# One-hot places of a routed group compared column by column in a fused attention and mixture-of-experts kernel

## The chip, the cores and the metric

The kernel runs on one core of one Trainium2 chip. The time is device microseconds from a launch's start to its end; of several runs the median is given. Beside the runs there is one profiled execution, from which all rows below come.

## What is computed

A linear attention over random features, and behind it a layer that sends each token to one of eight experts.

```python
batch, n_heads, seq, head_dim = (8, 8, 576, 64)      # 4608 tokens of 512
...
q_p, k_p = (phi(q_s), phi(k_s))                      # exp of projections on 128 features
kv = np.einsum('bhsm,bhsd->bhmd', k_p, v)
z = np.sum(k_p, axis=2)
num = np.einsum('bhsm,bhmd->bhsd', q_p, kv)
den = np.einsum('bhsm,bhm->bhs', q_p, z)[..., None] + 1e-06
...
logits = x @ w_gate
e_idx = np.argmax(logits, axis=1)                    # one expert a token
...
for e in range(E):
    mask = e_idx == e
    h = np.maximum(x[mask] @ w1[e], 0.0)
    ye = h @ w2[e]
    out[mask] = gate_w[mask, None] * eom[mask, e, None] * ye
```

## The kernel before

The 4608 tokens are worked in four groups of nine columns of 128 tokens (`NSC` = 4, `NC` = 9). For each group the attention of its eight pairs of heads is computed and written to the table `rows` in HBM, and then the group is routed: the expert of each token is found, and each token gets a rank among the tokens of its expert. The experts' work is done in items of 128 tokens of one expert. An item gathers its tokens' rows with an indirect DMA (`gx`), turns them (`xt`), multiplies by both weights of its expert (`hA`, `hB`, `out`) and scatters the result (`os`, `put`). Items of the groups that are routed are worked while the attention of the next group is still under way, so that the tensor engine goes back and forth between attention and items; only the items of the last group stand alone at the end.

The order of all steps is written out by hand in one list (`ORDER`), and each engine issues its instructions in that order. A step of several links (`route`, `ranks`, `places`, `table`, `assign`, `lists`) is a Python generator; each `yield` ends a link, and the list puts links of different steps and of the attention between them.

The steps around the change, all on VectorE save the two matmuls:
- `ranks` (L1036) makes `rank`, nine numbers a lane, in PSUM, in a bank that the group's routing holds (`inner`). The key of a token is a whole number for its block of 128, plus a fraction of a place.
- `places` (L1053) has three links: L1056 rounds the rank to the key (`keys`, in SBUF), L1058 subtracts the key, which leaves the token's place within its block, and L1060 compares it with `iota` (0 to 127, less a half of 127, fp16, in SBUF). The result is `place`: for each of the group's nine columns a matrix of 128 x 128 in fp16 that has one 1 a token. It is one instruction of 1152 elements, with `iota` read nine times over and each rank read 128 times.
- `table`, `assign`, `controls` set up which block of which expert goes to which item, and `lists` (L1144) compares the keys with the items' keys and makes `r_itc`.
- `pid` (L1283, `indices`) multiplies `place` by `r_itc` on the tensor engine, nine matmuls for each group that is routed so far; `gi` (L1320) and `oi` (L1326) are the lists of tokens that come out, for the gather and the scatter. `oi` is also what frees the bank of `pid`.
- At the end of the kernel two buffers for results are laid over `place` (L1421).

GpSimd works beside VectorE in the attention: L580 (`xlo`), L728 (`es`), L742 (`vs`) and L893 (`xs`), TENSOR_TENSORs from SBUF to SBUF, and it issues the gathers and scatters (L1565, L1664). VectorE's cast of `xs` is L889; L512 splits weights; L458, L459, L621 and L625 belong to the start of the kernel.

Of the kernel before, what the change touches and what calls it, by code (L numbers as in the profile page):

```python
# [16 lines left out]
ALU = mybir.AluOpType  # L17
# [5 lines left out]
P = 128  # L23
# [5 lines left out]
NC = 9  # L29
# [364 lines left out]
def attention_moe(ctx: ExitStack, tc: tile.TileContext, kqt, kqn, v, om, wg, w1, w2, cf, cm, ci, out):  # L394
    nc = tc.nc
# [11 lines left out]
    tri, ones, iota, ident16 = (cmt[:, i, :] for i in range(4))  # L407
# [20 lines left out]
    place = const.tile([P, NSC * NC, P], F16, name="place")  # L428
# [499 lines left out]
    def small(nm, sh, dt=F32):  # L928
        return sb.tile([P, *sh], dt, tag="r_" + nm, name="r_" + nm, bufs=1)
# [123 lines left out]
    def places(j):  # L1053

        rank, key = rt[j]["rank"], keys[:, j * NC : (j + 1) * NC]
        nc.vector.tensor_scalar(key, rank, WHOLES, -WHOLES, ALU.add, ALU.add)  # L1056
        yield
        nc.vector.tensor_tensor(out=rank, in0=rank, in1=key, op=ALU.subtract)  # L1058
        yield
        nc.vector.tensor_tensor(  # L1060
            out=place[:, j * NC : (j + 1) * NC, :],
            in0=iota.unsqueeze(1).broadcast_to([P, NC, P]),
            in1=rank.unsqueeze(2).broadcast_to([P, NC, P]),
            op=ALU.is_equal,
        )

    tabs = {}

# [270 lines left out]
    def routing(j):  # L1339


        def chain(name, links, gen, after, **kw):
            plan.chain((name, j), ("DVE",), links, lambda: gen(j), after=after, **kw)

        first = [("lga", H * (j + 1) - 1), ("const", "st"), ("const", "cf"), ("const", "cm")]
        if j:
            first += [("places", j - 1), ("scales", j - 1)]
        old = [g for g in range(NG) if GROUPS[g] < j]
        chain("route", 5, route, first)
        plan.add(("counts", j), ("PE",), lambda: counts(j), after=[("route", j)], bank=("e", ("pos", j), [NC + 1, NE]))  # L1350
        chain("ranks", 4, ranks, [("counts", j)] + [("table", g) for g in old], frees=[("pos", j)])
        chain("places", 3, places, [("ranks", j)])
        chain("gates", 2, gates, [("route", j)])
        plan.add(("gate_exps", j), ("ACT",), lambda: gate_exps(j), after=[("gates", j)])
        chain("weigh", 4, weigh, [("gate_exps", j)])
        plan.add(("scales", j), ("SP",), lambda: save_scales(j), after=[("weigh", j)], tiles=[("scales", j)])
# [414 lines left out]
```

## Time and profile before

| | |
|---|---|
| median of 3 runs | 644.57 us (643.44 to 647.48) |
| the profiled execution | 648.04 us |
| its span, first to last instruction | 646.2 us |
| tensor engine busy | 584.8 us, 91% of the span |
| VectorE busy | 407.2 us, 63%, 1115 instructions |
| ScalarE busy | 417.0 us, 65% |
| GpSimd busy | 362.1 us, 56%, 263 instructions |
| mean granted clock of the tensor engine | 0.978 |

A busy share is a mean over stages. The tensor engine's work is not spread evenly: in the first sixth of the span it often stands, and in the last items the chain of waits ends in a scatter. Times in the rows are us from the start of the span.

### The profile page before, as it was taken

What the parts mean: (1) busy time and instruction counts of PE and PEld (TensorE: products, weight loads), DVE (VectorE), ACT (ScalarE), POOL (GpSimd) and SP (SyncE); (2) the same over time, 40 slices, a digit from 0 to 9 for tenths busy, and PEclk for the clock granted to TensorE, in tenths of its full rate; (3) what the DMA queues carried; (4) which work ended last, traced back from release to release, by engine and by line L of the source; (5) the groups of instructions that cost most, each with busy time, mean ns of one, the idle gap of its engine ahead of it and who ended that gap; (6) DMA issues with size and microseconds to landing.
All of it is one profiled execution on the core that took longest, in us unless ns stands there. A gap on an engine that the chain in (4) does not pass through costs nothing. (4 is left out here: it accounts for less than half of the span.)

```text
span 646.2 us, 21319 instructions
## 1 busy us (share of the span) xinstructions
PE 584.8 (91%) x8412; PEld 452.7 (70%) x8412; DVE 407.2 (63%) x1115; ACT 417.0 (65%) x970; POOL 362.1 (56%) x263
## 2 busy tenths in 40 slices
PE   5899865999999898999989999999998899999983
PEld 4777754866777676777757776876776576767763
DVE  5988999957687687655757865564883620521052
ACT  5788997888888777878768577777521611521151
POOL 3887264388867856968657767858442211212111
PEclk9999997899999999999989999999999999999998
DMA  8696999999998987789999958558957744824570
GB/s 307 211 330 223 301 243 254 200 229 247 276 333 179 207 231 202 194 232 251 164 317 205 232 145 169 123 130 211 298 153 207 213 83 117 307 55 94 127 265 16
DMA packets 147759, 133.74 MB, mean 207 GB/s; under 512 B 104607, under 2 KB 128545, under 8 KB 146337
## 3 DMA queue, kind: packets, MB, share of 16 engines
q1 hardware_dynamic: 141632, 112.19, 68.0%
q0 software_dynamic: 5984, 19.72, 9.8%
q8 instruction: 82, 1.34, 0.9%
q14 instruction: 61, 0.49, 0.2%
HBM read 88.59 MB, written 19.30 MB: 167 GB/s over the span
## 5 line engine op out<-in xcount | busy, mean ns | idle before, releaser
L705 ACT ACTIVATE ef<-pp,nb 128x128 f32<-128x128 f32 x576 | 164.4, 389 | 48.2 <-DVE nb L699 36.1
L688 DVE TENSOR_REDUCE pp<-pp 128x3 f32<-128x384 f32 x192 | 104.8, 560 | 53.6 <-PE pp L670 48.9
L728 POOL TENSOR_TENSOR es<-ef,es 128x1152 f16<-128x1152 f32 x44 | 104.4, 2381 | 34.6 <-ACT es L726 13.1
L1599 PE MATMUL ph<-xt,w1h 128*128 128x128 f16 (+1 forms) x2048 | 121.7, 217 | 0.7 <-PE ph L1599 0.3
L1599 PEld LDWEIGHTS <-w1h 128*128 128x128 f16 x2048 | 113.3, 98 | 5.9 <-issue 0.8
L1565 POOL DMA_INDIRECT gx<-rows,gi x38 | 40.6, 1068 | 134.1 <-ACTq L1532 64.7
L1610 DVE SCALAR_TENSOR_TENSOR hl<-ph,hh 128x512 f16<-128x512 f32 (+1 forms) x76 | 50.4, 663 | 100.5 <-ACTq L1532 75.1
L1632 PEld LDWEIGHTS <-hh 128*128 128x128 f16 x560 | 51.6, 98 | 58.2 <-issue 4.0
L1606 ACT ACTIVATE hh<-ph 128x512 f16<-128x512 f32 (+1 forms) x76 | 44.7, 590 | 70.6 <-PE ph L1599 54.3
L580 POOL TENSOR_TENSOR xlo<-xt,xhi 128x1152 f16<-128x1152 f32 x24 | 57.5, 2398 | 25.0 <-ACT xhi L577 24.4
L1599 PE MATMUL ph<-xt,w1l 128*128 128x128 f16 (+1 forms) x1024 | 66.5, 217 | 2.2 <-issue 2.2
L1632 PE MATMUL po<-w2h,hh 128*128 128x512 f16 x240 | 62.6, 383 | 3.2 <-ACT w2h L507 2.9
L1632 PE MATMUL po<-w2h,hl 128*128 128x512 f16 x240 | 62.2, 382 | 0.5 <-DVE hl L1610 0.5
L1632 PE MATMUL po<-w2l,hh 128*128 128x512 f16 x240 | 61.6, 379 | 0.0
L1599 PEld LDWEIGHTS <-w1l 128*128 128x128 f16 x1024 | 58.4, 98 | 3.1 <-issue 3.0
L1675 ACT ACTIVATE os<-po,gx 128x512 f32<-128x512 f32 (+1 forms) x36 | 24.7, 686 | 48.4 <-PE po L1632 44.8
L893 POOL TENSOR_TENSOR xs<-xf,xs 128x576 f16<-128x576 f32 x32 | 40.9, 1283 | 20.9 <-DVE xs L889 9.5
L726 ACT CAST es<-ef 128x1152 f16<-128x1152 f32 x44 | 50.9, 1162 | 1.6 <-ACTq L1527 0.7
L1632 PEld LDWEIGHTS <-hl 128*128 128x128 f16 x280 | 27.1, 99 | 35.5 <-DVE hl L1610 3.5
L854 PE MATMUL pn<-kvs,et 128*128 128x81 f16 x768 | 39.3, 203 | 6.1 <-DVE oi L1326 3.1
L854 PEld LDWEIGHTS <-et 128*128 128x128 f16 x768 | 33.9, 98 | 10.2 <-issue 5.1
L670 PEld LDWEIGHTS <-xhi 64*128 64x128 f16 x864 | 26.5, 95 | 15.2 <-issue 10.0
(207 smaller groups left out, 1036.4 us busy)
## 6 DMA issues: line engine op xcount, KB each, us to landing
r<-w SPq DMA_DIRECT2D x10, 2048.0 KB
xn<-kqn SPq DMA_DIRECT2D x31, 576.0 KB
xt<-kqt SPq DMA_DIRECT2D x31, 576.0 KB
rawv<-v SPq DMA_DIRECT2D x32, 325.0 KB
rows<-xs SPq DMA_DIRECT2D x16, 576.0 KB
r<-w SPq DMA_DIRECT2D x8, 512.0 KB
ef<-w SPq DMA_DIRECT2D x2, 512.0 KB
et<-w SPq DMA_DIRECT2D x2, 512.0 KB
```

The lines of the kernel that those rows point to most:

```text
L580: plan.add(("lo", u, x), ("POOL",), lambda t0=t0, t1=t1: nc.gpsimd.tensor_tensor(out=xl(u)[:, t0:t1], in0=xt32(u)[:, t0:t1], in1=xh(u)[:, ...
L688: nc.vector.tensor_reduce(out=spare(g, 0)[:, i], in_=banks["pp", 2 * u + i, g][:, 0:3, :], op=ALU.min, axis=AX.X)
L705: nc.scalar.activation(ef(2 * u + i)[:, c, :], banks["pp", 2 * u + i, g][:, c % 3, :], AF.Exp, bias=nb(u)[:, i, c : c + 1], scale=-SK)
L726: nc.scalar.copy(es(slot_es(n))[:, 0], ef(n))
L728: nc.gpsimd.tensor_tensor(out=es(slot_es(n))[:, 1], in0=ef(n), in1=es(slot_es(n))[:, 0], op=ALU.subtract)
L854: nc.tensor.matmul(pn[:, c - c0, :], a[:, c, :], w[:, :, 0 if c < 4 else 1], start=(i == 0 and c == c0), stop=(c == NC - 1 and i == len(op ...
L893: nc.gpsimd.tensor_tensor(out=x[:, :, P + o : P + o + D], in0=xf(u)[:, :, 0:D], in1=x[:, :, o : o + D], op=ALU.subtract)
L1565: return nc.gpsimd.indirect_dma_start(out=gx(n), out_offset=None, in_=rows[0 : (j + 1) * NC * P], in_offset=bass.IndirectOffsetOnAxis(ap=t ...
L1599: nc.tensor.matmul(ph[:, f4, 0:w_], w[qd][:, kk, fo : fo + P], xt(n)[:, x, 0:w_], start=(z == 0 and f4 == 0 and x == 0), stop=(z == 1 and ...
L1606: nc.scalar.activation(hh(n)[:, sl, 0:w_], banks["ph", n, g][:, :, 0:w_], AF.Relu)
L1610: nc.vector.scalar_tensor_tensor(out=hl(n)[:, sl, 0:w_], in0=banks["ph", n, g][:, :, 0:w_], scalar=0.0, in1=hh(n)[:, sl, 0:w_], op0=ALU.ma ...
L1632: nc.tensor.matmul(po, x(n)[:, f, :], w[f // 2][:, f % 2, :], start=(f == 0 and a == 0), stop=(f == FC - 1 and a == 2))
```

## The change

The difference of rank and key is written to a new small tile in SBUF (`lane`), where it used to overwrite the rank in PSUM. The one compare of all nine columns becomes nine compares of one column each: `iota` is the only tensor that is read, and the place of each lane comes in as the instruction's scalar, one number a lane. The three links and their places in the order stay as they are; the nine compares are all in the third link.

```diff
--- before.py
+++ after.py
@@ -1055,14 +1055,11 @@
         rank, key = rt[j]["rank"], keys[:, j * NC : (j + 1) * NC]
         nc.vector.tensor_scalar(key, rank, WHOLES, -WHOLES, ALU.add, ALU.add)
         yield
-        nc.vector.tensor_tensor(out=rank, in0=rank, in1=key, op=ALU.subtract)
-        yield
-        nc.vector.tensor_tensor(
-            out=place[:, j * NC : (j + 1) * NC, :],
-            in0=iota.unsqueeze(1).broadcast_to([P, NC, P]),
-            in1=rank.unsqueeze(2).broadcast_to([P, NC, P]),
-            op=ALU.is_equal,
-        )
+        lane = small("place", [NC])
+        nc.vector.tensor_tensor(out=lane, in0=rank, in1=key, op=ALU.subtract)
+        yield
+        for c in range(NC):
+            nc.vector.tensor_scalar(place[:, j * NC + c, :], iota, lane[:, c : c + 1], None, ALU.is_equal)
 
     tabs = {}
```

## Rows read from the trace of the kernel before

**Rows 1.** Busy time by stage: us, then busy (instructions) of PE, PEld, DVE, ACT, POOL; PEclk.

```profile
104.00:107.00 3.00, 0.24 (x3) 0.14 (x3) 2.93 (x13) 1.07 (x2) 2.48 (x2) 0.74 1.34 177
...
120.00:480.00 360.00, 343.99 (x5336) 262.83 (x5336) 249.08 (x697) 269.41 (x616) 258.52 (x170) 1.00 0.89 217
```

**Rows 2.** The compare: ns min/median/max, starts; VectorE's timeline (start us, us, instruction), three of four.

```profile
L1060 DVE TENSOR_TENSOR place<-cmt,rt x4: 1353/1353/1355, 100.8 to 479.2; 128x1152 f16<-128x1152 f16 x4
...
100.78 1.35 DVE L1060 TENSOR_TENSOR place<-cmt,rt 128x1152 f16<-128x1152 f16 x1
...
228.04 1.35 DVE L1060 TENSOR_TENSOR place<-cmt,rt 128x1152 f16<-128x1152 f16 x1
...
364.55 1.35 DVE L1060 TENSOR_TENSOR place<-cmt,rt 128x1152 f16<-128x1152 f16 x1
```

**Rows 3.** VectorE's timeline: TENSOR_SCALARs with a lane's scalar, and their followers.

```profile
106.01 0.22 DVE L1195 TENSOR_SCALAR rt<-cft,r_tot 128x8 f32<-128x8 f32 x1
106.14 0.56 DVE L688 TENSOR_REDUCE pp<-pp 128x3 f32<-128x384 f32 x1
...
485.79 0.43 DVE L1186 TENSOR_SCALAR ef<-ef,cft 128x864 f16<-128x864 f16 x1
486.14 0.16 DVE L1216 SCALAR_TENSOR_TENSOR r_lim<-state,rt 128x8 f32<-128x8 f32 x1
```

**Rows 4.** Durations of one cast; then timelines of VectorE and GpSimd around 248 and 18.

```profile
L889 DVE CAST xs<-xf x32: 478/484/2381, 28.2 to 471.5; 128x576 f16<-128x576 f32 x32
...
248.34 2.38 DVE L889 CAST xs<-xf 128x576 f16<-128x576 f32 x1
...
248.00 2.37 POOL L728 TENSOR_TENSOR es<-ef,es 128x1152 f16<-128x1152 f32 x1 [1.60 <-ACT es L726]
...
17.72 0.61 DVE L458 TENSOR_SCALAR wgh<-wgr 128x256 f16<-128x256 f32 x1
18.36 1.58 DVE L459 SCALAR_TENSOR_TENSOR wgl<-wgr,wgh 128x256 f16<-128x256 f32 x1
...
18.26 1.41 POOL L625 TENSOR_TENSOR sqt<-sqt 128x576 f32<-128x576 f32 x1
```

**Rows 5.** GpSimd's timeline beside the four compares.

```profile
101.78 4.69 POOL L580 TENSOR_TENSOR xlo<-xt,xhi 128x1152 f16<-128x1152 f32 x2
...
227.29 2.39 POOL L728 TENSOR_TENSOR es<-ef,es 128x1152 f16<-128x1152 f32 x1
231.64 2.38 POOL L580 TENSOR_TENSOR xlo<-xt,xhi 128x1152 f16<-128x1152 f32 x1 [1.96 <-ACT xhi L577]
...
365.29 2.38 POOL L580 TENSOR_TENSOR xlo<-xt,xhi 128x1152 f16<-128x1152 f32 x1
367.63 1.43 POOL L742 TENSOR_TENSOR vs<-rawv,vs 128x650 f16<-128x650 f32 x1
...
477.57 1.00 POOL L1664 DMA_INDIRECT out<-os,oi  x1 [0.30 <-issue]
```

**Rows 6.** Timelines of the tensor engine and VectorE: lists, `pid` and waits.

```profile
111.08 0.98 PE L854 MATMUL pn<-kvs,et 128*128 128x81 f16 x12 [3.14 <-DVE oi L1326]
...
233.04 0.45 DVE L1164 TENSOR_TENSOR r_itc<-r_eq,rt 128x288 f16<-128x288 f16 x1
...
233.79 0.60 PE L1287 MATMUL pid<-r_itc,place 128*128 128x16 f16 x18
...
367.58 0.17 DVE L868 TENSOR_SCALAR den<-pn 128x5 f32<-128x5 f32 x1 [0.44 <-PE pn L861]
...
370.20 0.66 DVE L1164 TENSOR_TENSOR r_itc<-r_eq,rt 128x486 f16<-128x486 f16 x1
...
371.33 0.84 PE L1287 MATMUL pid<-r_itc,place 128*128 128x18 f16 x27
```

**Rows 7.** The tensor engine's timeline at 331, and that stretch by stage (as rows 1).

```profile
331.38 1.96 PE L1632 MATMUL po<-w2h,hh 128*128 128x512 f16 x4 [2.94 <-ACT w2h L507]
...
331.00:334.00 3.00, 2.62 (x7) 0.83 (x7) 2.64 (x3) 3.00 (x4) 0.00 (x0) 0.50 1.14 330
```

## The prediction

> **What bounds the kernel now.** I read four views, in this order. First the table by stage (busy time of each engine in a stretch), to see which engine sets the pace where the change sits. From 120 to 480 us the tensor engine is busy 343.99 of 360.00 us [rows 1]: whatever holds it up in that stretch or ahead of it has almost no idle time later in which to be made up. Ahead of it, where the first of the four groups is routed, it is the other way round: from 104 to 107 us VectorE is busy 2.93 of 3.00 us and the tensor engine 0.24 [rows 1]. Second, the instructions that write `place`: the compare runs four times, 1353 to 1355 ns, never stretched [rows 2]. Third, VectorE's order of time, for what small instructions cost in a row [rows 3]. Fourth, GpSimd's order of time beside it, because some VectorE instructions have two very different durations and GpSimd's rows explain which [rows 4, 5].
>
> **What goes.** One TENSOR_TENSOR of 1152 elements, at 1.35 us a group [rows 2]. Neighbours on VectorE overlap: the row of 0.22 us at 106.01 is followed at 106.14 [rows 3], 0.09 before its end. So the old compare holds its queue for about 1.35 - 0.08 = 1.27 us. The subtraction stays one instruction of 9 elements; that it writes SBUF and no longer PSUM I cost at nothing: it stands in the same place of the queue, and its result is first read by the instruction that also reads it now.
>
> **What comes, with nothing in its way.** Nine TENSOR_SCALARs of 128 fp16 elements, each with a scalar of its lane. Two rows of that kind exist. With 8 elements the next instruction starts 0.13 us later; with 864 fp16 elements, both sides in SBUF, 0.35 us later [rows 3]. The slope is (0.35 - 0.13) / 856 = 0.26 ns an element, against 1.35 us / 1152 = 1.17 ns in the old compare: the one-source form runs about four elements for each one of the two-source form. A compare of 128 elements is 0.13 + 0.03 = 0.16 us, nine are 1.44 us, against 1.27: +0.17 a group. The bounds: if the fixed part were the 0.09 between 106.14 and its neighbour's end, nine would be about 1.08 (-0.19 a group); if they ran at the old 1.17 ns, 9 x (0.13 + 0.15) = 2.52 (+1.25 a group). I take 1.44, since the 864-element row has operands, scalar and type of the new ones.
>
> [...]
>
> **What is in its way.** The form that is quick is also the one that stops for GpSimd. The cast of `xs` (one source, SBUF to SBUF) takes 478 to 484 ns as a rule and 2381 at most; the longest starts at 248.34 and ends at 250.72, and GpSimd's TENSOR_TENSOR ran from 248.00 to 250.37 [rows 4]. The cast ended 0.35 after it, having waited for its end. The old compare, one of whose two inputs is in PSUM, ran 1354 ns four times, with GpSimd busy in three of them [rows 2, 5]. Nine TENSOR_SCALARs from SBUF to SBUF should behave as the cast does. And each asks anew: around 18 us a TENSOR_SCALAR ended at 18.33, GpSimd's next operation had started at 18.26, and the VectorE instruction of 18.36 ended at 19.94, 0.27 after GpSimd's end at 19.67 [rows 4]. A GpSimd operation that stands ready gets in between two VectorE instructions. [...]
>
> *First group, 100.78.* A GpSimd operation ends at 101.8 and two more, 4.69 us together, follow without idle time, to 106.47 [rows 5]. One or two compares get in at 101.8, one or two at about 104.1, the other five or six after 106.47: 106.5 + 6 x 0.16 + 0.1 for GpSimd's own delay = 107.6, where the old one let go at 100.78 + 1.27 = 102.05. That is +5.5 us. Behind it VectorE queues everything up to the list of places, the tensor engine's next work waits for VectorE (3.14 us at 111.08 [rows 6]), and VectorE has no idle time there [rows 1]. All 5.5 reach the end. If VectorE kept the port for all nine it would be 101.8 + 1.44 - 102.05 = +1.2.
>
> *Second group, 228.04.* GpSimd's operation ends at 229.68; the next starts at 231.64 after 1.96 idle [rows 5]. The nine run from 229.68 to 231.12, against 229.31: +1.8. `r_itc` ended at 233.49 and the tensor engine's `pid` began at 233.79 [rows 6], so 0.3 is covered and +1.5 is left.
>
> *Third group, 364.55.* GpSimd runs without a gap until 365.3, 367.67 and 369.06 [rows 5]. By the same alternation the last five or six compares come after 369.06: 369.06 + 0.96 + 0.1 = 370.1 against 365.82, +4.3. Cover: 0.44 idle at 367.58, and `r_itc` ended at 370.86 where `pid` began at 371.33, 0.47 [rows 6]. The tensor engine stands 3.4. [...] The 2.62 us of work in that stretch would have been half of it at full clock, 1.3; I add 1.0, as the work behind `pid` waits for others in part. Together +4.4. If VectorE kept the port: 365.3 + 1.44 - 365.82 = +0.9, all of it covered.
>
> *Fourth group, 479.2.* GpSimd's last operation ends at 478.57 [rows 5], ahead of the compares: +0.2.
>
> **The sum.** 5.5 + 1.5 + 4.4 + 0.2 = 11.6 us. The profiled execution took 648.04 us, so the changed one would take 659.6; it lies 3.5 above the median of the runs, 644.57, and for the median the sum gives 656.2.
>
> **The rivals.**
> - *VectorE keeps the port for all nine*, since the next compare is already lined up when one ends: 1.2 + 1.5 + 0 + 0.2 = +2.9, 647.5. For it: the wait of one cast ended only 0.35 after GpSimd's, so a waiting VectorE does get in. Against it: 18.26 [rows 4].
> - *Mixed*, the port is lost in one of the two runs of GpSimd work and kept in the other, or lost for one operation: +5 to +7, about 650.5.
> - *Not quick at all*: the nine run at the old 1.17 ns an element and never meet GpSimd. +1.25 on VectorE; first group 1.25, second 1.25 - 0.3, third 1.25 - 0.91, fourth 1.25: +3.8, 648.4. Against it: the 864-element row.
> - *Hidden*: the compares wait, but the tensor engine has other work, or they don't wait and cost +0.17: 644.9. Against it: the 3.14 us wait at 111.08 [rows 6].
> - *Faster*: the port is no matter for these nine, and their fixed part is 0.09, so that a row of nine takes 1.08 us. The gain is 0.19 in the first and fourth group, where VectorE is waited for, and nothing in the others: -0.4, 644.2. It decides from a spacing of 1.27 / 9 = 0.141 us a compare, without waits. [...]
>
> **How the numbers follow.** Alternation 0.52 (own range 651.5 to 659.5, from one more or one fewer GpSimd operation waited for at the third group and the clock term left out), VectorE keeps the port 0.17, mixed 0.10, not quick 0.05, hidden 0.07, faster 0.05, longer than 659.5 (a compare caught by still another GpSimd operation) 0.04. A measurement of this kernel can tell about 1% from no change, so slower means over 651.0. That is the alternation, the longest cases and about a quarter of the mixed: 0.58. Faster by over 1% needs 6.4 us, and no case gives it: 0.02. Within 1% is the rest, 0.40. The range 646.5 to 659.5 leaves out the hidden and the faster case and the longest, 0.16.
>
> **What would show it.** Right: in the first and third group single compares of over 2 us whose ends lie 0.1 to 0.4 us behind the end of a GpSimd TENSOR_TENSOR, the others 0.16 apart; in the second only the first compare long (about 1.7 us); in the fourth none. The tensor engine's wait at the first group's `pn` behind `oi` comes 5 to 6 us later, and it stands about 3 us before the third group's `pid`, with a granted clock of 0.50 behind it. Wrong: nine compares in a row with at most one long one (the port is kept), or spacings near 0.28 and none long (not the quick form), or spacings under 0.141. The forecast also fails if VectorE's delay in the first group doesn't move the tensor engine's work after 120 us, or if the shifted order meets GpSimd elsewhere, for example at the casts of `xs`, so that what is gained or lost there outweighs the compares.

## The result, and the profile after

The changed kernel takes 654.67 us (median of 6 runs, 646.94 to 659.84); the kernel before, run beside it, 645.99 us (6 runs, 642.92 to 647.71). The ratio is 1.0106, with a 95% interval of 1.0056 to 1.0155. In another set of runs it was 658.02 us against 647.76, ratio 1.0158 (1.0103 to 1.0213). It is slower, by 1 to 1.6%; the forecast was 656.2 us. A ratio leaves out runs over 1.5% above the fastest of their kernel, so it need not be the quotient of the two medians.

The first profiled execution of the changed kernel was the shortest of its six (646.94 us), so a second was taken, of 659.48 us. "The second profile" below is that one, with its companion of the kernel before (646.48 us). In the other tables, too, one profile is one execution, and where in it a time falls differs by some us from one to the next.

First the compares, grouped by line (duration in ns, min/median/max), of the first profile and of the second; they answer [rows 2].

```profile
L1062 DVE TENSOR_SCALAR place<-cmt,r_place x36: 241/244/2417, 100.4 to 480.6; 128x128 f16<-128x128 f16 x36
...
L1062 DVE TENSOR_SCALAR place<-cmt,r_place x36: 240/246/2417, 102.6 to 491.8; 128x128 f16<-128x128 f16 x36
```

The median compare takes 0.24 us, ten times less than the longest. What nine cost with nothing in their way is to be seen in the fourth group, in VectorE's timeline of the first profile (start us, us):

```profile
479.25 1.55 DVE L1062 TENSOR_SCALAR place<-cmt,r_place 128x128 f16<-128x128 f16 x9
480.72 0.35 DVE L1122 SCALAR_TENSOR_TENSOR r_mine<-r_mine,r_within 128x192 f32<-128x192 f32 x1
```

The next instruction starts 1.47 us after the first compare: 0.163 us a compare, against 0.16 in the forecast, and +0.2 us a group over the old one. Now the first group of the second profile, VectorE and then GpSimd, to be held against [rows 5]:

```profile
102.56 1.35 DVE L1062 TENSOR_SCALAR place<-cmt,r_place 128x128 f16<-128x128 f16 x1
103.83 2.41 DVE L1062 TENSOR_SCALAR place<-cmt,r_place 128x128 f16<-128x128 f16 x1
106.49 2.36 DVE L1062 TENSOR_SCALAR place<-cmt,r_place 128x128 f16<-128x128 f16 x1
...
101.48 2.38 POOL L728 TENSOR_TENSOR es<-ef,es 128x1152 f16<-128x1152 f32 x1 [4.29 <-ACT es L726]
103.81 2.38 POOL L580 TENSOR_TENSOR xlo<-xt,xhi 128x1152 f16<-128x1152 f32 x1
106.43 2.36 POOL L580 TENSOR_TENSOR xlo<-xt,xhi 128x1152 f16<-128x1152 f32 x1 [0.24 <-ACT xhi L577]
```

GpSimd's operations end at 103.86, 106.19 and 108.79; the three long compares end at 103.91, 106.24 and 108.85. Each stands through one operation of GpSimd, to 0.05 or 0.06 us behind its end, and then the next operation of GpSimd, already lined up, gets in before the next compare: at 103.81 against 103.83. So not one short compare runs between the first long one and the second; two run at 106.2, because GpSimd itself waited 0.24 us there for ScalarE. The third group of the same execution:

```profile
370.04 0.88 DVE L1062 TENSOR_SCALAR place<-cmt,r_place 128x128 f16<-128x128 f16 x1
370.83 2.42 DVE L1062 TENSOR_SCALAR place<-cmt,r_place 128x128 f16<-128x128 f16 x1
373.17 1.46 DVE L1062 TENSOR_SCALAR place<-cmt,r_place 128x128 f16<-128x128 f16 x1
375.04 2.21 DVE L1062 TENSOR_SCALAR place<-cmt,r_place 128x128 f16<-128x128 f16 x1
...
369.58 1.28 POOL L893 TENSOR_TENSOR xs<-xf,xs 128x576 f16<-128x576 f32 x1 [1.37 <-DVE rt L1120]
370.82 2.38 POOL L580 TENSOR_TENSOR xlo<-xt,xhi 128x1152 f16<-128x1152 f32 x1
373.16 1.42 POOL L742 TENSOR_TENSOR vs<-rawv,vs 128x650 f16<-128x650 f32 x1
374.74 1.00 POOL L1661 DMA_INDIRECT out<-os,oi  x1 [0.16 <-issue]
375.74 1.45 POOL L742 TENSOR_TENSOR vs<-rawv,vs 128x650 f16<-128x650 f32 x1
```

Four compares are caught, not three: the one of 375.04 starts while GpSimd issues a scatter and ends at 377.25, behind the second L742 (377.19). What the tensor engine makes of it, second profile, its timeline with its waits, at `pid` and `pn` of the first group and at `pid` of the third ([rows 6]):

```profile
114.88 0.41 PE L1284 MATMUL pid<-r_itc,place 128*128 128x16 f16 x9 [2.90 <-DVE r_itc L1161]
118.43 0.98 PE L854 MATMUL pn<-kvs,et 128*128 128x81 f16 x12 [3.14 <-DVE oi L1323]
...
380.70 0.50 PE L670 MATMUL pp<-omh,xhi 64*128 64x128 f16 x5 [4.15 <-DVE xf L872]
...
382.05 0.87 PE L1284 MATMUL pid<-r_itc,place 128*128 128x18 f16 x27 [0.21 <-DVE r_itc L1161]
```

Before the third `pid` it stands 4.15 + 0.21 us, the first of them for an `xf` that stands behind the compares in VectorE's order. The table by stage (as [rows 1]) shows the end of this stand and what follows, first of the changed kernel, then of the kernel before beside it:

```profile
379.00:385.50 6.50, 4.59 (x53) 2.82 (x54) 5.82 (x29) 1.63 (x3) 1.22 (x2) 0.51 0.37 99
...
379.00:385.50 6.50, 6.50 (x139) 5.69 (x137) 4.04 (x12) 5.01 (x15) 3.60 (x3) 1.00 0.74 207
```

The granted clock is 0.51 in this stretch, in which a stand of over 4 us ends, and 1.00 in the kernel before. What the third group costs in all can be read between two matmuls ahead of the stand and behind the slow stretch, first in the kernel before, then in the changed one (second profiles):

```profile
365.71 0.63 PE L854 MATMUL pn<-kvs,et 128*128 128x81 f16 x12
...
383.33 1.06 PE L1599 MATMUL ph<-xt,w1l 128*128 128x128 f16 x16
...
372.25 0.63 PE L854 MATMUL pn<-kvs,et 128*128 128x81 f16 x12
...
395.04 1.06 PE L1596 MATMUL ph<-xt,w1l 128*128 128x128 f16 x16
```

That is 17.62 us before and 22.79 after, 5.2 more. The first profiles give the same, 17.62 (366.65 to 384.27) and 22.80 (363.08 to 385.88).

### The profile page after: what moved, and what is told of

The parts are those of the page before. It is cut to its first block, busy times and chain, and to the rows that moved or that the text cites. A ratio compares the mean times of both kernels' runs of the same rounds, so it can differ in the third digit from the quotient of the medians.

```text
span 645.0 us, 21352 instructions
## 1 busy us (share of the span) xinstructions
PE 584.0 (91%) x8412; PEld 453.0 (70%) x8412; DVE 415.1 (64%) x1147; ACT 417.5 (65%) x970; POOL 360.2 (56%) x263
## 5 line engine op out<-in xcount | busy, mean ns | idle before, releaser
L580 POOL TENSOR_TENSOR xlo<-xt,xhi 128x1152 f16<-128x1152 f32 x24 | 57.5, 2399 | 24.6 <-ACT xhi L577 24.0
```

Of the source, the lines that this page charges most:

```text
L580: plan.add(("lo", u, x), ("POOL",), lambda t0=t0, t1=t1: nc.gpsimd.tensor_tensor(out=xl(u)[:, t0:t1], in0=xt32(u)[:, t0:t1], in1=xh(u)[:, ...
```

## The experiments

**before_look** and **after_look** are the two kernels as they are, for a profile of each on one chip.

> The kernel before, for its spread and for where its clock falls from one execution to the next. Port theory (the nine compares lose time because GpSimd's operations get between them): 643 to 648 us, every compare of 1152 elements 1.35 us, and one stretch of 3 to 4 us at half the clock behind 120 us. Spread theory (the 1% lies in where the clock falls, and either kernel can draw it): some executions near 655 us.

646.18 us (10 runs), ratio to the other runs of the same kernel 0.9982 (0.995 to 1.0015): a ratio of 1.002 is nothing here. None of the ten came near 655 us, which the spread theory wanted (of the 29 runs beside them one took 654.52). Around 331 us (329 to 336) its granted clock was 1.00, where [rows 7] show 0.50, so that fall comes and goes between executions.

> The changed kernel once more, for a profile of a typical execution. Port theory: 650 to 658 us; in groups one to three single compares of 0.9 to 2.4 us that end 0.05 to 0.1 us behind a GpSimd operation, the rest 0.24 us long and 0.16 apart; the tensor engine's lists matmul of the first group 3 us later than before, that of the third group behind a stand of 3 us or more with half the clock after it. Spread theory: the same waits of the compares, but the tensor engine no later at 400 us than in the kernel before, as in the first profile.

658.02 us, 1.0158 (1.0103 to 1.0213); its rows stand above. The first list came 7.1 us later than in the kernel before, not 3.

**nine_plain** keeps the nine instructions and makes them slow: TENSOR_TENSORs with the place in PSUM.

```diff
-            out=place[:, j * NC : (j + 1) * NC, :],
...
+        for c in range(NC):
+            nc.vector.tensor_tensor(
+                out=place[:, j * NC + c, :], in0=iota, in1=rank[:, c : c + 1].broadcast_to([P, P]), op=ALU.is_equal
+            )
```

> Nine compares of one column each as in the change, but as TENSOR_TENSORs with the place still in PSUM and read as a broadcast operand, so not the quick form. Port theory: no compare over 0.35 us with GpSimd busy or not; nine take about 9 x 0.22 = 2.0 us, 0.7 more than the one; 645 to 648 us. Instruction theory (it is the number of instructions that costs): the time of the changed kernel, 652 to 656 us, and a delay of the first group's list like that of the change, 3 us.

649.93 us, 1.003 (1.000 to 1.0061). The 36 compares, grouped by line:

```profile
L1061 DVE TENSOR_TENSOR place<-cmt,rt x36: 277/279/289, 101.7 to 480.2; 128x128 f16<-128x128 f16 x36
```

Not one is stretched, though GpSimd ran beside them (an `es` from 100.32 to 102.70 and an `xlo` behind it, while the first group's nine ran from 101.66 to 103.53). So the number of instructions alone costs 0.3%, at most 0.6 (the time is above the 645 to 648 us that was expected), and being caught is not a matter of nine.

**one_in_sbuf** keeps the one instruction and moves only its second source to SBUF.

```diff
+        lane = small("place", [NC])
+        nc.vector.tensor_tensor(out=lane, in0=rank, in1=key, op=ALU.subtract)
...
-            in1=rank.unsqueeze(2).broadcast_to([P, NC, P]),
+            in1=lane.unsqueeze(2).broadcast_to([P, NC, P]),
```

> The other part of the change alone: the places stand in SBUF, the compare stays one TENSOR_TENSOR of 1152 elements, now with both inputs in SBUF. Port theory with the waits of a whole instruction: it meets GpSimd once a group, 1.0 us in the first, 1.7 in the second, 0.8 in the third, 0 in the fourth, so durations near 2.4, 3.0, 2.1 and 1.35 us; 645.5 to 648.5 us. Rival (only the quick form meets GpSimd, the place of the scalar doesn't matter): 1.35 us in all four, 644 to 647 us.

648.2 us, 0.9995 (0.9964 to 1.0025). The compares, grouped by line; VectorE and GpSimd at the longest:

```profile
L1061 DVE TENSOR_TENSOR place<-cmt,r_place x4: 1359/2184/2511, 102.7 to 478.9; 128x1152 f16<-128x1152 f16 x4
...
102.71 2.51 DVE L1061 TENSOR_TENSOR place<-cmt,r_place 128x1152 f16<-128x1152 f16 x1
...
101.62 2.38 POOL L728 TENSOR_TENSOR es<-ef,es 128x1152 f16<-128x1152 f32 x1 [4.30 <-ACT es L726]
103.96 3.48 POOL L580 TENSOR_TENSOR xlo<-xt,xhi 128x1152 f16<-128x1152 f32 x1
```

With the lane in SBUF the slow form is caught too, 2.51 us instead of 1.36, and GpSimd's next operation is 1.1 us longer than its usual 2.38. It is caught in three groups of four, but one instruction is caught once, and that costs nothing that is measured. What makes the change dear is both together, sources in SBUF and nine chances. Whether the quick form has a part in it is open: nine TENSOR_TENSORs with both sources in SBUF were not run.

**only_first**, **only_third** and **only_second** make the change in one group and leave the old compare in the others; the diff of the first, the others with 2 and 1 for 0:

```diff
+        if j == 0:
+            lane = small("place", [NC])
+            nc.vector.tensor_tensor(out=lane, in0=rank, in1=key, op=ALU.subtract)
+            yield
+            for c in range(NC):
+                nc.vector.tensor_scalar(place[:, j * NC + c, :], iota, lane[:, c : c + 1], None, ALU.is_equal)
+        else:
...
```

> Nine quick compares in the first group alone, the old compare in the other three. Theory of places (each group's delay counts by what stands behind it): the first group's list comes 3 us late if GpSimd has one operation ready and 5.5 if it has two; by 160 us about 2.8 of that is made up, as in the kernel with one compare in SBUF, so 645.5 to 649.5 us. Theory of my forecast (the tensor engine makes nothing up behind 120 us): all of it reaches the end, 650 to 653.

650.2 us, 1.0069 (1.0031 to 1.0107): +4.5 us. That lies at the lower end of what the forecast's own theory gives, 650 to 653, and above the 649.5 of the other. Three compares of 1.35, 2.41 and 2.35 us, as above.

> Nine quick compares in the third group alone. Theory of places: the compares are stretched by three or four GpSimd operations, the third list is 2.5 to 5 us late, the tensor engine stands ahead of it and runs at half its clock for 3.4 or 6.8 us behind it, and nothing is made up afterwards: 650 to 653 us, more than half of the change's loss. Rival (the loss comes from the first group, which stands at the head of everything): 645 to 647.5 us.

652.69 us, 1.009 (1.006 to 1.0121): +5.8 us. Again four long compares; the tensor engine stands 4.14 and 0.63 us. The tensor engine's timeline behind it, first of this kernel, then the same `po` matmuls of the kernel before (second profile):

```profile
377.27 0.87 PE L1294 MATMUL pid<-r_itc,place 128*128 128x18 f16 x27 [0.63 <-DVE r_itc L1171]
...
378.16 1.91 PE L1639 MATMUL po<-w2h,hh 128*128 128x512 f16 x4
379.87 1.91 PE L1639 MATMUL po<-w2h,hl 128*128 128x512 f16 x4
...
371.20 1.03 PE L1632 MATMUL po<-w2h,hh 128*128 128x512 f16 x4
372.06 1.03 PE L1632 MATMUL po<-w2h,hl 128*128 128x512 f16 x4
```

The same four matmuls take 1.91 instead of 1.03 us, and in two rows the lag grows from 378.16 - 371.20 = 6.96 to 379.87 - 372.06 = 7.81 us. The stretch from 376.4 to 383.2 us, 6.8 us, had a granted clock of 0.50, as had 369.9 to 376.7 us in the first profile of the changed kernel; the fall of [rows 7], first profile of the kernel before, lasted 3.4 us (330.7 to 334.1). Between the two matmuls named in the section on the result (here 367.48 and 391.38) it is 23.90 us, 6.3 more than before.

> Nine quick compares in the second group alone. Theory of places: one compare is caught by the one GpSimd operation at hand, 1.2 to 1.8 us; the second list comes 1 to 2 us late, and little of it is made up: 646 to 648.5 us, the smallest of the three groups. Rival (the groups' losses don't add up; what decides is whether the clock falls): as much as the first or the third group alone, 649 us or more.

643.23 us, 0.995 (0.9917 to 0.9983): faster, where a small loss had been expected. It is a small gain: the medians of all runs, 643.23 against 645.29, differ by 0.3% alone, so the traces must bear it out. The one long compare is there, 1.81 us. Where the time comes from: VectorE and GpSimd around the casts of `xs`, first in the second profile of the kernel before, then here.

```profile
246.95 1.81 DVE L889 CAST xs<-xf 128x576 f16<-128x576 f32 x1
...
250.34 2.35 DVE L889 CAST xs<-xf 128x576 f16<-128x576 f32 x1
...
246.95 1.45 POOL L742 TENSOR_TENSOR vs<-rawv,vs 128x650 f16<-128x650 f32 x1
249.98 2.37 POOL L728 TENSOR_TENSOR es<-ef,es 128x1152 f16<-128x1152 f32 x1 [1.58 <-ACT es L726]
...
253.62 0.27 PE L827 MATMUL kv<-cmt,kvs 128*128 128x128 f16 x2 [1.44 <-DVE kvs L811]
```

```profile
245.50 0.48 DVE L889 CAST xs<-xf 128x576 f16<-128x576 f32 x1
...
247.75 0.48 DVE L889 CAST xs<-xf 128x576 f16<-128x576 f32 x1
...
246.38 1.46 POOL L742 TENSOR_TENSOR vs<-rawv,vs 128x650 f16<-128x650 f32 x1
248.35 2.37 POOL L728 TENSOR_TENSOR es<-ef,es 128x1152 f16<-128x1152 f32 x1 [0.52 <-ACT es L726]
```

In the kernel before two casts start with or just behind an operation of GpSimd and take 1.81 and 2.35 us, and the tensor engine waits 1.44 us for the `kvs` behind them. Here both casts start ahead of GpSimd's operation, take 0.48 each, and that wait is gone. From the `kv` matmuls of `vs` ahead of it to this one the tensor engine takes 5.62 us in the kernel before (248.00 to 253.62) and 3.55 here (246.37 to 249.92), 2.1 less. The same two casts are free in the first, short profile of the changed kernel and caught in its second, long one (1.82 and 2.29 us).

**cast_moved** tests that: the kernel before, with only the first of the two casts put three links ahead. **second_and_cast** adds this to only_second.

```diff
-... xf.17.5:0 xf.17.0:0 mx.38.1 gx.8<17 xf.17.5:1 xf.17.0:1 advance.1:9 sqa.23 xf.17.0 xf.17.5 put.6<17 xh.16
+... xf.17.5:0 xf.17.0:0 xh.16 mx.38.1 gx.8<17 xf.17.5:1 xf.17.0:1 advance.1:9 sqa.23 xf.17.0 xf.17.5 put.6<17
```

> The kernel before, with one move and no other change: the cast of `xs` (L889) that was caught at 246.95 us for 1.81 us goes three links ahead in VectorE's order, into the idle time in front of the bias of 245.23 (0.72 us there, with GpSimd's TENSOR_TENSOR over at 244.2 and the next one not before 246.95). None of the change's compares is in it. If the gain of the kernel with the new compares in its second group alone (643.23, 0.995) came from the two casts that were not caught: this cast takes 0.48 us, the next one of 250.34 comes about 1.5 us sooner, ahead of GpSimd's operation at 249.98, and takes 0.48 too, the tensor engine doesn't wait for `kvs` (L811, 1.44 us) at 252, and the time is 2 to 3.5 us under the kernel before, a ratio of 0.9945 to 0.997. If that gain came from elsewhere (the compares, or an order that is shifted later): a ratio of 0.999 to 1.002, with or without caught casts.

> The new compares in the second group alone, and the same cast moved as in the kernel beside it. If the casts are the whole of the gain of the second group alone, the two do not add: the casts take 0.48 us in both, the first of the nine compares is still caught behind GpSimd's operation (1.8 us), and the time is that of the cast moved alone or up to 1 us longer, a ratio of 0.995 to 0.998. If the second group's compares gain something of their own, the gains add: 0.990 to 0.9925.

643.97 us, 0.9964 (0.9929 to 0.9999), and 641.72 us, 0.9956 (0.9924 to 0.9988). In cast_moved the casts take 0.62 and 0.48 us, the wait for `kvs` is gone, and the stretch of 5.62 us takes 3.55 again (251.25 to 254.80):

```profile
248.20 0.62 DVE L889 CAST xs<-xf 128x576 f16<-128x576 f32 x1
...
252.62 0.48 DVE L889 CAST xs<-xf 128x576 f16<-128x576 f32 x1
...
254.80 0.27 PE L827 MATMUL kv<-cmt,kvs 128*128 128x128 f16 x2
```

The two gains do not add (that would be 0.9914, just below the last interval), and second_and_cast takes the same 3.55 us at this place (245.66 to 249.21). So most of what only_second gains is that its order lets these casts go first. That the new compares give it something of their own is not excluded: the intervals overlap. That its tensor engine was 1.2 us ahead at 156 us already (154.88 against 156.11 at the same matmul), before its only edit runs, can only be the difference between two executions.

**third_moved** and **all_moved** keep the change and move the compares out of GpSimd's way: the third group's right behind its difference; in all_moved also the first group's behind `lists.0` and the second's behind `assign.1`, with `pid` waiting for `places` in place of `lists`.

```diff
-weigh.2:1 places.2:1 kv.25.0 nb.26.1:0 assign.2:1 ... nb.26.1 places.2 ex.53.1 lo.27.0 rows.11 os.14
+weigh.2:1 places.2:1 places.2 kv.25.0 nb.26.1:0 assign.2:1 ... nb.26.1 ex.53.1 lo.27.0 rows.11 os.14
```

> The change, with the third group's nine compares issued right behind the subtraction, ahead of the cast of xs, where GpSimd stands in wait for that cast; nothing else moved. Port theory: no compare of the third group over 0.5 us, its list on time within 1 us, no half clock behind it; 5 us less than the change, 649 to 652 us. Instruction theory: the time of the change.

650.07 us, 1.0028 (0.999 to 1.0066). The third group's nine, in VectorE's timeline:

```profile
367.85 1.56 DVE L1062 TENSOR_SCALAR place<-cmt,r_place 128x128 f16<-128x128 f16 x9
```

None is caught, and no fall of the clock follows (1.00 from 360 to 390 us); the first group's three are caught as ever (101.15 to 108.1 us for all nine).

> The change, with the nine compares of the first, second and third group issued at places of VectorE's order where GpSimd has nothing in SBUF to do: the first behind the group's lists, the second behind its assignment, the third as in the run before. The same instructions, as many as in the change. Port theory: single compares wait 0.5 us at most, and 0.17 us a group is all that is left: 645 to 648.5 us, as the kernel before. Instruction theory: the time of the change, 652 to 658 us.

649.67 us, 1.0041 (1.0007 to 1.0076). The first and third group's are free; the second group's, at its new place, met an L580 and had one of 2.37 us:

```profile
235.04 2.37 DVE L1062 TENSOR_SCALAR place<-cmt,r_place 128x128 f16<-128x128 f16 x1
...
234.92 2.44 POOL L580 TENSOR_TENSOR xlo<-xt,xhi 128x1152 f16<-128x1152 f32 x1 [3.58 <-ACT xhi L577]
```

The time is above the 645 to 648.5 us expected, with one compare still caught. About two thirds of the loss go with the catches. What is left is no gain: nothing here shows the quick form ahead of the old one.

**second_old** is all_moved with the old compare, at its old place, in the second group (`if j != 1:` around the new ones).

> As the run with all three moved, but the second group keeps its old compare at its old place, since its moved compares were caught for 2.4 us. Port theory: no compare of any group waits over 0.5 us; the time of the kernel before within 0.3%, 644.5 to 648 us. Rival (what was left over in that run, 0.4%, is the 0.17 us a group and the moving itself): 648.5 to 650 us again.

647.73 us, 1.0079 (1.0039 to 1.0119); the medians, 647.73 and 645.29, differ by 0.4%. No compare is caught at all, and yet it isn't faster than all_moved: a miss. In its profile the casts of `xs` are caught again (2.39 us at 247.72, 1.59 at 251.70), where those of all_moved are free (0.48 us each, at 250.66 and 252.90); that would explain why it isn't faster than all_moved. It doesn't explain why it is slower than the kernel before, whose casts are caught too. That stays open.

## Why the prediction was right, and where not

- **One compare, 0.16 us; not the slow form.** Right: 0.163, and 1.47 us for nine. The rivals "faster" and "not quick at all" fall with the measured 0.163.
- **GpSimd gets in between two compares.** Right: 103.81 against 103.83, again at 370.82 (against 370.83) and 373.16 (against 373.17). "Port" in the forecast and the expectations names no part that a trace shows: the rows show only that instructions of the two engines waited for each other. "VectorE keeps the port" falls: several compares in one group stood, 0.9 to 2.4 us each. nine_plain and one_in_sbuf together show that here it hangs on where the operands lie: nine with the place in PSUM were never caught (277 to 289 ns), one with both sources in SBUF was (up to 2.51 us).
- **First group, +5.5 us.** The stall was right: `pid` at 114.88 against 107.80 in the second profile of the kernel before, 7.1 later, of which 1.5 is a later start of the compares (102.56 against 101.06); 5.6 is left. In the first, short profile only two compares of this group were caught, because GpSimd's third operation had waited 1.68 us for ScalarE, and `pid` came only 3 us late (110.60): the compares stood through one operation less, as in the mixed rival.
- **"All 5.5 reach the end."** Not settled. only_first measures the term at +4.5, with an interval of 2.0 to 6.9 us that has 5.5 in it. The traces seem at first to say that half is made up. The tensor engine's timeline from `pid` to a later matmul: the kernel before in its second profile, the same kernel in its first, and the later matmul of the changed kernel (second profile, its `pid` at 114.88):

```profile
107.80 0.41 PE L1287 MATMUL pid<-r_itc,place 128*128 128x16 f16 x9 [2.06 <-DVE r_itc L1164]
...
156.11 0.19 PE L833 MATMUL kv<-wgh,kvf 128*128 128x32 f16 x1 [0.88 <-ACT kvf L836]
...
107.53 0.41 PE L1287 MATMUL pid<-r_itc,place 128*128 128x16 f16 x9 [2.17 <-DVE r_itc L1164]
...
154.04 0.19 PE L833 MATMUL kv<-wgh,kvf 128*128 128x32 f16 x1 [0.87 <-ACT kvf L836]
...
160.34 0.19 PE L833 MATMUL kv<-wgh,kvf 128*128 128x32 f16 x1 [0.21 <-ACT kvf L836]
```

The stretch takes 48.31 us in the one profile of the kernel before and 45.46 in the changed kernel, 2.9 less. But it takes 46.51 in the other profile of the kernel before, 45.25 in only_second (109.63 to 154.88), whose first group has the old compare, and 47.11 in only_first (112.20 to 159.31), which has the delay. Executions differ here by 3 us whether there is a delay to make up or not, so nothing is shown to be made up.

- **Second group, +1.5.** The first compare is long (1.22 to 1.81 us), the others short, as forecast. The tensor engine felt 1.0 us of it in only_second, where it waits that long before the second `pid` (235.18), and nothing in the second profile of the changed kernel, where `pid` follows without a wait (241.60). But alone this group gains: only_second, -3.2 us (-5.4 to -1.1). The step that failed is the silent one, that nothing else changes when the order shifts. The last sentence of the prediction named the casts of `xs` as a risk; I gave them no price, and they are worth some 2.3 us (cast_moved, 0.9964; 0.1 to 4.6 us), 2.1 by the tensor engine's rows. In the changed kernel that gain comes and goes: its first profile has it, its second hasn't.
- **Third group, +4.4.** Under-sized: +5.8 (3.9 to 7.8) in only_third, and by the tensor engine's rows 5.2 in both profiles of the changed kernel and 6.3 in only_third. The stand was 4.4 to 4.8 us, not 3.4, as a fourth long compare came of GpSimd's scatter and second L742, in all three profiles. The prediction had one more operation at this group in its range, not in its sum; these two operations stand in the old trace too (369.20 and 370.22), and I stopped reading two rows too early. The clock term, 1.0, was an estimate, from the 2.62 us of work and the clock of 0.50 between 331 and 334 us in [rows 7]; that such a fall follows a stand of 3.4 us no run shows. What the three profiles show is a clock of 0.50 or 0.51 about the end of stands of 4.13 to 4.15 us, and the term was about right: the lag grew by 0.85 us over one row of four matmuls, and what the rows leave beside the stand is 0.8 to 1.5.
- **Fourth group, +0.2.** Right.
- **The sum, 11.6 us.** The three groups alone come to 4.5 + 5.8 - 3.2 = 7.1 us, and the whole change to 1.0106 x 645.99, +6.8 (3.6 to 10.0), or 1.0158 x 647.76, +10.2 (6.7 to 13.8). So 11.6 is above the first interval and within the second, likely too much: the third group's term was too low, the second's too high, and the casts, which can give back 2.1, stood at nothing. That these errors go against each other is luck, and so is part of the median's being close to 656.2: the kernel before ran at 645.99 and 647.76, not at 644.57.

## What to carry to other kernels

Where instructions of two engines are seen to wait for each other, as those of VectorE and GpSimd here, ask of a quicker form not only what it takes alone but what it waits for, and how often: one slow compare with a source in PSUM was never stretched (1353 to 1355 ns), one with both in SBUF was caught once (up to 2.51 us), and nine quick ones two to four times in the first and third group (0.9 to 2.4 us each), where GpSimd's operations came one behind the other. Before such a change read the neighbour's queue to the end of the stall, and put the burst where that queue is empty. Look also for other instructions of the same kind that the shift will put ahead of or behind the neighbour's work. And before a delay is called made up further on, hold the same stretch of several executions beside each other: here it differed by 3 us with no delay at all.

## What the runs showed of the hardware

- A GpSimd operation that stood ready started 0.01 to 0.02 us ahead of the next VectorE instruction of a row without gaps, so that the row was cut after a single instruction (103.81 against 103.83, 370.82 against 370.83, 373.16 against 373.17).
- A VectorE compare of 0.24 us that started 0.3 us into the issue of an indirect DMA on GpSimd stood through the rest of it and the next operation, 2.21 us in all (375.04; 2.21 also in the first profile and in only_third).
- A TENSOR_TENSOR of VectorE with both sources in SBUF, which alone takes 1.36 us, took 2.51 beside GpSimd, and GpSimd's operation 3.48 instead of 2.38.
- Whether two casts of 0.48 us take 1 or 4 us together hung on which of two engines started first, by less than 1 us (0.48 and 0.48 in only_second, 1.81 and 2.35 in the second profile of the kernel before); it changed between kernels whose edits lie elsewhere, and between executions of one.
